# A gated linear attention and a SoLU layer in one kernel: a new order of the work, five states added on VectorE, five squares halved on GpSimd, the last unit in halves

## The chip, the cores and the metric

The kernel runs on one core of a Trainium2 chip. The metric is the time of one execution in microseconds as the device measures it. Runs of one kernel differ by about half a per cent, so the median of several is given. Besides, one execution was profiled: the profile gives the span from the first to the last instruction, and what each engine did in it. The engines are TensorE (in the rows PE, its weight loads PEld), VectorE (DVE), ScalarE (ACT), GpSimd (POOL) and SyncE (SP), which only issues transfers.

## The reference

Two layers. The first goes through 768 steps for each of 4 batches and 8 heads, with a state of 48 x 48 for each head:

```python
for t in range(S):
    kt, vt, rt, wt = (k[:, :, t], v[:, :, t], r[:, :, t], w[:, :, t])
    cur = np.einsum('bhd,bhe->bhde', u[None] * kt, vt)
    y[:, :, t] = np.einsum('bhd,bhde->bhe', rt, state + cur)
    state = wt[:, :, :, None] * state + np.einsum('bhd,bhe->bhde', kt, vt)
```

The second takes the 3072 rows of 384 numbers that come out and computes

```python
h = x @ w_in                       # 384 -> 1024
solu = h * softmax(h)
ln = (solu - mean) / np.sqrt(var + 1e-06) * g_ln
return ln @ w_out                  # 1024 -> 384
```

## The kernel before

The sequence is cut into 6 chunks of 128 steps. One chunk of one batch is a *unit*: there are 24, unit i being chunk i // 4 of batch i % 4. Every unit goes through the same stages, and each stage is a small function with a short name.

The attention of a unit: `LW`, `LK`, `LR`, `LV` load w, k, r and v (192 KB each). `lw` takes the logarithm of w (ACT), `cum` adds it up over the steps with two matmuls, `ex` takes the exponential in place in PSUM (ACT), and `kp` multiplies k and r by it (DVE). `krk` and `krr` turn the two on TensorE and `kr` copies them to SBUF, or `kt` does both with a transfer that turns (units 12, 13 and 15 to 23). `M` makes the scores of the chunk, `m` masks them (mostly DVE). `p`, `q` (POOL), `dg` (DVE) and `dv` (POOL) make the term with u. `Y` collects the output of the attention in PSUM: the term with u (through a matmul on the identity in units marked `i`; in units marked `n` DVE adds it in `y`), the old state, and the scores times v. `y` copies it to SBUF.

The state: `S` collects in one PSUM bank the sum of the logarithms, the old state (a matmul on the identity with 384 columns) and k times v; `et` takes an exponential of the sums (ACT, 8 columns), `st` multiplies the bank by it (DVE) and writes the new state as bf16. `Y` and `S` of the next chunk of that batch read it.

The second layer: `X` and `xT` turn y (or `xt`, a transfer). `H` makes the hidden product, transposed, with 24 matmuls of 128 columns (for units 17 to 20 by rows, with `ht` turning afterwards). `e` takes the exponential (ACT), `he` multiplies (DVE), `hq` squares (ACT, 1024 columns). `Oa` and `Ob` make the output in one bank: for each of 8 blocks one matmul of he with 386 columns, one of e with 2 columns, one of hq with 1 column, the last two being sums for the normalization. In units with an `ea` word POOL adds the two halves of e first, and 4 of the 8 matmuls of e fall away. `qm` (DVE), `lv`, `rs` (ACT) make the factor of each row, `o` applies it (ACT or DVE), `out` stores 192 KB. Unit 23 goes through the hidden layer in two halves (`HA`, `EA`, `DA`, `QA`, then `HB`, `EB`, `DB`, `QB`). `hot` is a number of matmuls whose result nobody reads.

The order is written out by hand, in one string of some 890 words, `ORDER`. A loop at the end goes through the words and calls the stage. `InOrder` keeps the instructions of each engine in the order of the words, and also the transfers of SP and ACT among themselves. So a word sets the place of its instruction in its engine's queue; an instruction that waits holds up everything behind it on that engine. The part after the dot says the engine (`a` ACT, `d` DVE, `p` POOL; for loads `g` POOL's queue, `a` ACT's, none SP's), or the PSUM bank (0 to 7). Buffers are rings: 7 for the loads, 10 for lw and vb, 6 for kp, kr and dv, 4 for most others, 3 for p and q.

Of the kernel before, what the change touches and what calls it, by code (L numbers as in the profile page):

```python
# [8 lines left out]
F32 = mybir.dt.float32  # L9
# [15 lines left out]
hot10.1 LV1 LR5 LK6.a dv0 LK5.g m2.d LV2.a LO1 M3.0 S0.7 q3 gw2.a gw3.a hot1.4 LI1 q1 lw6 krk1.6 cum4.2 et0 LV4  # L25
m3.d p2 st0 cum6.0 dg3 gw0.a cum5.4 ex4 S3.7 gw1.a p4 kp4 q2 dv3 krr1 ex6 dg1 LV5.g krk4.3 krr4 ex5 vb1.a Y0.i2
kp6 kr4.d y0.a LI2 et3 X0.2 krk6.3 st3 p6 kr1.a vb2.a LW8 xT0.a kp5 krr6 LI0.a dg2 M1.0 krk5.7 krr5 kr6.a m1.d
S1.2 dv1 M4.4 dv2 Y3.i3 S2.6 gw4.a LK7 gw7.a et2 kr5.d LW7.g et1 m4.d hot1.7 y3.a q4 gw6.a Y1.i3 M6.0 gw5.a st2
Y2.i5 y1.a y2.a vb5.a mn0.4 X2.7 wi0.a vb4.a st1 m6.d wi1.p LR7.g M5.2 X1.0 S5.1 xT2.a S4.6 et5 p5 lw7 LR8.g dg4
ce4.d LK8 LV7 et4 ce2.d wi2.a xT1.d st5 LW10.a st4 X3.5 m5.d LR10.a cum7.0 mc0 ex7 xT3.a ce1.d H0.6 dv4 H1.2 kp7  # L30
LK9.g H3.0 e0 lw8 e1 ce0.d LK10.a he0 he1 lw10 H2.6 ce7.d hq0.a ce3.p krk7.5 ce5.p e3 LV9 e2 LK11 hq1.a ce6.d
Oa0.3 q6 he3 vb7.a krr7 Ob0 LW9.g LV6.g Y4.i4 q5 LV8.g LR9.a he2 dg5 LW11 cum10.1 cum8.6 y4.a Oa1.0 qm0 ex10 lv0
rs0 kr7.d ex8 kp10 LW13.g Ob1 krk10.4 o0.a hq3.a p8 kp8 p7 dv5 Y5.n5 qm1 LR11.g y5.d lv1 M7.2 X4.6 LW15.a m7.d
q7 krr10 LW17 dg7 kr10.d xT4.a q8 dg6 rs1 lw11 p10 Oa3.5 o1.a cum11.6 dg8 hq2.a H4.2 LW12 LR12.a ex11 lw9 kp11
out0 S7.0 et7 Ob3 dv7 Y7.n1 vb6.a out1 cum9.6 LR17 LK15.g Oa2.4 qm3 st7 vb8.p e4 Ob2 he4 lv3 dv6 LK14.g krk8.0
S6.2 X5.3 LK12.a LV10 krr8 LV12.g ex9 lw13 y7.d rs3 o3.a hq4.a kp9 lw12 qm2 Y6.i5 lv2 xT5.d X7.7 krk11.6 LV11
# [10 lines left out]
lv8 vb13.p q13 e11 kp18 dv14 rs8 S15.2 o8.a S13.3 st12 e12 Oa9.0 dv15 he11 et15 lw21 LW20 Y15.n6 hq11.a et13
dg13 LV21 he12 Ob9 LV23.g LV19.g p18 st15 M13.4 LW23 y15.d qm9 dv13 kt16 cum21.1 hq12.a ex21 H10.6 lv9 p16 m13.d
st13 lw19 kp21 Y13.i4 Oa11.3 e10 rs9 o9.a out7 he10 q18 cum19.1 Ob11 dg18 qm11 lw20 Oa12.7 Ob12 ex19 LR22 q16
y13.a kp19 hq10.a M16.1 dg16 S14.5 lv11 Y14.n6 rs11 LV20.g X13.4 LV22.g out8 qm12 lv12 p17 m16.d xT13.d y14.d  # L50
o11.a lw22 S16.0 vb17.p et14 q17 dg17 rs12 st14 o12.a LR23 vb18.a cum20.1 p19 et16 ex20 ea10.p H13.3 q19 e13
xt15 dv17 lw23 kt17 dv16 H15.6 st16 kp20 he13 Oa10.5 xt14 M17.0 kt18 dg19 dv18 e15 cum22.2 Ob10 out9 ex22 vb22.p
Y16.i4 ea13.p he15 kp22 y16.a hq13.a p22 qm10 H14.6 vb20.p M18.3 m17.d p20 S18.2 q20 lv10 m18.d ea15.p e14 kt19
et18 rs10 Y17.n1 o10.a Oa13.0 y17.d kt20 p21 X16.4 Ob13 xT16.a st18 out11 q22 M19.3 xt17 he14 H16.1 hq15.a
Y18.n5 vb23.a e16 m19.d hq14.a Oa15.7 vb19.a dg20 kt21 y18.d qm13 out12 Ob15 ea14.p dv19 M20.4 q21 S17.3 lv13
he16 m20.d qm15 dv20 et17 hq16.a lv15 H17.1 rs13 out10 e17 M21.5 st17 xt18 rs15 ea16.p Oa14.4 m21.d Ob14 he17
o15.a o13.a cum23.5 qm14 LK23 Y20.n3 ex23 Y19.n7 lv14 y20.d y19.d H18.0 rs14 o14.a kp23 kt22 M22.3 e18 dg22
X20.2 vb21.p S19.7 m22.d xT20.a Oa16.6 Y21.n5 ht17 et19 p23 sv17 he18 xt19 hq17.a dv22 H20.2 e20 dg21 Ob16 st19
dv21 y21.d he20 hq18.a H19.0 qm16 e19 sv18 Y22.n4 Oa17.7 y22.d he19 kt23 Ob17 X22.5 sq17 M23.3 xT22.d qm17 m23.d
ht18 xt21 ht20 hq19.a lv16 Oa18.2 lv17 rs16 Ob18 ht19 q23 dg23 H21.0 o16.d sv19 Y23.n3 dv23 out15 hq20.a e21  # L60
y23.d H22.4 Oa20.6 out13 e22 Ob20 sq18 ea21.p Oa19.3 Ob19 he21 rs17 he22 hq21.a sq20 Oa21.1 o17.d sv20 out16
# [39 lines left out]
def kernel(  # L101
# [132 lines left out]

    u_bc = consts.tile([C, H, D], BF16)
# [305 lines left out]

    def hidden_half(part):
# [75 lines left out]
    def scaled_out(i, x):  # L618
        o_ps, rs, o = live[i]["o_ps"], rs_t[i % NWK], o_t[i % NWK]
        if x == "d":  # L620
            dve.tensor_scalar(out=o, in0=o_ps[:, :DM], scalar1=rs, scalar2=None, op0=MULT)
        else:
            act.activation(out=o, in_=o_ps[:, :DM], func=COPY, scale=rs)

    def store(i, x):
        c, b = units[i]
        queue[x].dma_start(out=out[b * S + c * C:b * S + (c + 1) * C, :], in_=o_t[i % NWK])
# [8 lines left out]
        H=hidden, e=hidden_exp, he=hidden_mul, ea=hidden_add, hq=hidden_square, Oa=output_a, Ob=output_b,  # L636
# [39 lines left out]
```

## Time and profile before

| | us |
|---|---|
| median of 3 runs | 145.75 |
| lowest and highest of them | 144.95, 146.58 |
| the profiled execution | 145.05 |
| its span | 143.2 |
| busy: PE, DVE, ACT, POOL | 127.6, 124.0, 122.2, 117.2 |

The rows of a timeline give the start, the time, the engine, the line, the operation, what is written and read (buffer numbers left out), the shapes and a count; in brackets stands the idle time of the engine ahead of it and what ended it. Nearly every row has line 86, since all instructions are made in one helper there; go by the names. Groups have a count, the busy time, the mean of one in ns, and the idle time ahead of them with what ended it. A view of waits gives who waited for whom: the sum, how often, the longest.

### The profile page before, as it was taken

To read this page: it belongs to the slowest core of one execution; us is meant where nothing else is said; L and a number is where in the kernel's file an instruction comes from. 1 tells how busy PE (TensorE), PEld (TensorE's weight loads), DVE (VectorE), ACT (ScalarE), POOL (GpSimd) and SP (SyncE) were. 2 spreads that over 40 slices of the span, in tenths; PEclk is the share of its full clock that TensorE was granted. 3 is DMA by queue.
4 is the path that set the end of the run, shared out by engine and by line. 5 is a ranking of instruction groups with operands and counts; after the bars stand their busy time and mean duration, and the time that the engine had idled before them with its cause. 6 is when DMAs were issued, how large, how long until landed. Compare 5 with 4: busy or idle time off the path is not lost.

```text
span 143.2 us, 4784 instructions
## 1 busy us (share of the span) xinstructions
PE 127.6 (89%) x1886; PEld 94.5 (66%) x1886; DVE 124.0 (87%) x206; ACT 122.2 (85%) x254; POOL 117.2 (82%) x150
## 2 busy tenths in 40 slices
PE   0597956988999999999999999996999999999980
PEld 0145445556967878678987797786778566687750
DVE  6048879979999999999999999999699999888480
ACT  3658799979999999999999989995787887887962
POOL 7999999999999999999999999999994753326000
PEclk9999999999999999999999999999999999999998
DMA  4999999999995999999998999996977863985325
GB/s 93 277 297 347 313 287 381 384 267 240 287 299 118 250 273 314 255 263 163 211 268 215 271 201 252 195 256 99 169 165 80 223 128 79 142 213 180 115 80 197
DMA packets 86488, 31.67 MB, mean 221 GB/s; under 512 B 80153, under 2 KB 84258, under 8 KB 86466
## 3 DMA queue, kind: packets, MB, share of 16 engines
q1 hardware_dynamic: 69330, 20.62, 66.6%
q0 software_dynamic: 2432, 7.47, 16.4%
q10 hardware_dynamic: 14704, 3.28, 10.5%
q8 instruction: 14, 0.23, 0.7%
q14 instruction: 8, 0.07, 0.1%
HBM read 22.03 MB, written 4.72 MB: 187 GB/s over the span
## 4 chain that ended last, share of the span: by engine, by line
PE 51%; POOL 21%; ACT 8%; issue 7%; DVE 5%; DMA 4%; ACTq 0%; POOLq 0%; DVEq 0%
PE ps L86 51%; DMA xT<-y 4%; POOL kr_in L86 4%; POOL p L86 4%; POOL q L86 3%; POOL dv L86 2%; POOL v_in L86 2%; ACT hq L86 2%; POOL w_in L86 2%; ACT e L86 2%; DVE he L86 1%; DVE o L86 1%; ACT o L86 1%; ACT ps L86 1%; DVE m L86 1%
## 5 line engine op out<-in xcount | busy, mean ns | idle before, releaser
L86 PE MATMUL ps<-w,he 128*128 128x386 bf16 (+1 forms) x192 | 42.5, 324 | 0.0
L86 PE MATMUL ps<-xT,win_sb 128*128 128x128 bf16 x480 | 29.6, 219 | 1.4 <-DMA xT<-y 1.2
L86 PEld LDWEIGHTS <-win_sb 128*128 128x128 bf16 x480 | 27.4, 98 | 3.0 <-DMA xT<-y 1.3
L86 POOL TENSOR_TENSOR dv<-vb,dg 128x384 bf16<-128x384 bf16 x24 | 19.8, 829 | 11.8 <-DVE dg L86 8.6
L86 DVE TENSOR_TENSOR kp<-ps,kr_in 128x768 bf16<-128x768 f32 x24 | 22.7, 953 | 6.9 <-DMA kr_in<-in_r_dram 3.8
L86 ACT ACTIVATE e<-ps 128x1024 bf16<-128x1024 f32 (+1 forms) x25 | 24.6, 987 | 4.8 <-PE ps L86 3.8
L86 DVE TENSOR_TENSOR m<-ps,keep 128x1024 bf16<-128x1024 f32 x22 | 26.7, 1218 | 0.9 <-PE ps L86 0.9
L86 DVE TENSOR_TENSOR he<-ps,e 128x1024 bf16<-128x1024 f32 (+1 forms) x21 | 24.5, 1170 | 3.0 <-ACT e L86 2.8
L86 PE MATMUL ps<-one_col,hq 128*128 128x1 bf16 x160 | 26.1, 163 | 0.0
L86 POOL TENSOR_TENSOR p<-kr_in 128x384 bf16<-128x384 f32 x24 | 23.9, 1005 | 0.1
L86 POOL TENSOR_TENSOR q<-p,u_bc 128x384 bf16<-128x384 bf16 x24 | 21.8, 916 | 0.3
L86 PEld LDWEIGHTS <-he 128*128 128x128 bf16 x192 | 18.3, 96 | 4.0
L86 ACT ACTIVATE hq<-he 128x1024 bf16<-128x1024 bf16 (+1 forms) x20 | 20.7, 1033 | 0.0
L86 ACT ACTIVATE ps<-ps 128x768 f32<-128x768 f32 x24 | 19.0, 800 | 1.5 <-PE ps L86 1.4
L86 PEld LDWEIGHTS <-hq 128*128 128x128 bf16 x160 | 14.1, 96 | 8.8
L86 PE MATMUL ps<-inv_col,e 128*128 128x2 bf16 x104 | 17.1, 164 | 0.0
L86 ACT ACTIVATE lw<-w_in 128x384 bf16<-128x384 f32 x24 | 12.3, 519 | 4.2 <-DMA w_in<-in_w_dram 4.2
L86 PEld LDWEIGHTS <-kp 128*128 128x128 bf16 x184 | 12.3, 101 | 4.2 <-DVE kp L86 1.9
L86 PEld LDWEIGHTS <-kr 64*128 64x128 bf16 (+1 forms) x272 | 10.2, 95 | 5.3 <-issue 2.1
L86 DVE TENSOR_REDUCE dg<-q 128x8 f32<-128x384 bf16 x24 | 12.9, 543 | 0.0
L86 DVE TENSOR_TENSOR st<-ps,et 128x384 bf16<-128x384 f32 x20 | 10.8, 551 | 1.4 <-ACT et L86 1.4
L86 POOL DMA_DIRECT2D v_in<-in_v_dram x12 | 10.9, 905 | 0.0
(97 smaller groups left out, 284.9 us busy)
## 6 DMA issues: line engine op xcount, KB each, us to landing
out_dram<-o SPq DMA_DIRECT2D x24, 192.0 KB, 2.7
w_in<-in_w_dram SPq DMA_DIRECT2D x12, 192.0 KB, 5.6
kr_in<-in_k_dram SPq DMA_DIRECT2D x12, 192.0 KB, 5.9
v_in<-in_v_dram POOLq DMA_DIRECT2D x12, 192.0 KB, 4.9
kr_in<-in_r_dram POOLq DMA_DIRECT2D x11, 192.0 KB, 4.5
v_in<-in_v_dram SPq DMA_DIRECT2D x11, 192.0 KB, 4.3
kr_in<-in_r_dram SPq DMA_DIRECT2D x9, 192.0 KB, 4.0
wout_f<-in_moe_w_out_dram SPq DMA_DIRECT2D x2, 768.0 KB, 7.1
```

Source lines behind the costliest of these rows:

```text
L86: made = make(*args, **kwargs)
```

## The change

Five things, of which the first is most of the diff.

1. `ORDER` is replaced as a whole. No load, store or turning transfer changes its queue, nor its place among the others of its queue. What changes is how the words of the engines stand among each other and among the transfers, and for some words the engine or the bank. The y of unit 0 stands ahead of the scores of unit 1, with the copy of u and its matmul at the very start. VectorE loses two `o` (six before, four after) and one `xT` to ScalarE; GpSimd gets two more `vb` and gives one cast of w_in to ScalarE; the other copies change places with no change of the counts. The `ea` of unit 14 falls away.
2. In units 10, 13, 15, 16 and 19 (`S` marked `n`) the matmul that adds the old state falls away. `st` has two instructions on VectorE in its place: it adds the bank and the old state into a new f32 tile in SBUF, and multiplies that by et.
3. In units 10, 13, 14, 16 and 22 a new word `qa` lets GpSimd add the second half of hq to the first, in place (512 columns), and 4 of the 8 matmuls of hq fall away.
4. Unit 23's second output goes through its four blocks three times, first he, then e, then hq, where it took the three of a block together.
5. Unit 23's `o` is made in two halves, one on ScalarE and one on VectorE, and stored by two transfers of 96 KB, one on ScalarE's queue and one on SyncE's.

```diff
-LU0 LR3.g LW3.a LW1.a LW2.g lw3 LR0.a cum3.0 LG0 ih0 ex3 LW0 gs0.7 LK3 LR2.g hot1.2 LV0.g ik0 LK0 lw1 lw0 LV3.g
-gc0 cum0.4 LK2.a us0.6 p0 lw2 LW5.g ex0 kp3 LR1 kp0 cum1.0 cum2.2 krk3.7 krr3 uc0 ex2 q0 ex1 kp2 LK1 LR6.g kp1
-krk0.6 LW4 krr0 krk2.5 krr2 kr0.a lw4 LR4.g vb0.a kr2.d vb3.a p1 M0.3 p3 LO0 LW6 dg0 M2.5 kr3.a LK4 m0.d lw5
...
+LR3.g LU0 LW3.a us0.1 LW2.g LW1.a lw3 uc0 ih0 LR0.a LG0 LW0 LK3 LR2.g cum3.3 ex3 lw0 lw1 gs0.0 LK0 LV0.g cum0.6
+LK2.a kp3 ex0 lw2 LR1 cum1.3 gc0 cum2.1 LK1 kp0 krk3.0 ex1 krr3 krk0.6 ex2 hot1.5 krr0 LW4 LO0 kp2 kr3.a kp1
+LV3.g p0 LW5.g q0 ik0 LW6 kr0.a vb0.a M3.1 LR6.g krk2.5 LK4 krr2 LR4.g p1 vb3.a dg0 M0.3 m3.d kr2.a S0.0 krk1.2
+dv0 krr1 S3.7 q1 M2.5 m0.d LK5.g m2.d p2 kr1.a Y0.i1 q2 p3 lw4 q3 LV1 et0 st0 LR5 hot1.3 y0.a M1.5 m1.d gw1.a
...
+kp19 xt14 X13.3 m16.d qm12 xT13.a lv12 qa10.p S14.4 et16 cum20.0 dg17 st16 H13.2 rs12 o12.a ex20 et14 e13 dg18
+H15.6 LV19.g dv17 ea13.p q20 vb21.a kp20 M17.0 Oa10.5 he13 e15 p19 kt18 cum22.2 st14 ex22 q19 Y16.i4 he15 hq13.a
...
+dv20 S19.n2 y19.d LK23 kt22 qm14 hq16.a cum23.5 dg21 vb22.p et19 Y20.n4 ht17 ex23 qa16.p ea16.p xt19 lv14 rs14
...
+rs21 o19.d out18 HB23.7 o21.d EA23 EB23 qa22.p DA23 out19 qm20 QA23.a lv20 out21 Oa22.0 DB23 Ob22 qm22 QB23.d
+lv22 Oa23.4 rs20 rs22 Ob23 o20.d qm23 o22.a lv23 rs23 o23.a out22 out20 out23.h
...
+    sn_t = ring("sn", 2, [C, H, D], F32)
...
-        s_ps = L["s_ps"] = bank([C, DM + H], F32, x, "s_ps")
+        s_ps = L["s_ps"] = bank([C, DM + H], F32, x[-1], "s_ps")
...
-        if c > 0:
+        L["apart"] = x[0] == "n"
+        if c > 0 and not L["apart"]:
             st = st_t[b][(c - 1) % 2]
             pe.matmul(s_ps[:, :DM], lhsT=ident, rhs=st.rearrange("p h e -> p (h e)"), start=False, stop=False,
                       skip_group_check=True)
...
-        dve.tensor_mul(out=st_t[b][c % 2], in0=live[i]["s_ps"][:, :DM].rearrange("p (h e) -> p h e", h=H), in1=et)
+        total = live[i]["s_ps"][:, :DM].rearrange("p (h e) -> p h e", h=H)
+        if live[i]["apart"]:
+            dve.tensor_add(out=sn_t[i % 2], in0=total, in1=st_t[b][(c - 1) % 2])
+            total = sn_t[i % 2]
+        dve.tensor_mul(out=st_t[b][c % 2], in0=total, in1=et)
...
+    paired = {int(word[2:].split(".")[0]) for word in ORDER.split() if word.startswith("qa")}
+
+    def square_add(i, x):
+        hq = hq_t[i % NWK]
+        pool.tensor_add(out=hq[:, :KF // 2, :], in0=hq[:, :KF // 2, :], in1=hq[:, KF // 2:, :])
...
+    split = "out23.h" in ORDER.split()
...
+        if i == NU - 1 and part and split:
+            for f in range(KF // 2, KF):
+                pe.matmul(o_ps[:, :DM + 2], lhsT=he[:, f, :], rhs=w2[:, f, :], start=False, stop=False,
+                          skip_group_check=True)
...
+            return
...
-            pe.matmul(o_ps[:, DM + 2:], lhsT=hq[:, f, :], rhs=one_col[:, :1], start=False, stop=(f == KF - 1),
-                      skip_group_check=True)
+            if i not in paired:
+                pe.matmul(o_ps[:, DM + 2:], lhsT=hq[:, f, :], rhs=one_col[:, :1], start=False, stop=(f == KF - 1),
+                          skip_group_check=True)
+            elif f % 2 == 0:
+                pe.matmul(o_ps[:, DM + 2:], lhsT=hq[:, f // 2, :], rhs=one_col[:, :1], start=False,
+                          stop=(f == KF - 2), skip_group_check=True)
...
+        if i == NU - 1 and split:
+            act.activation(out=o[:, :DM // 2], in_=o_ps[:, :DM // 2], func=COPY, scale=rs)
+            dve.tensor_scalar(out=o[:, DM // 2:], in0=o_ps[:, DM // 2:DM], scalar1=rs, scalar2=None, op0=MULT)
+            return
...
+        if x == "h":
+            act.dma_start(out=rows[:, :DM // 2], in_=o_t[i % NWK][:, :DM // 2])
+            sp.dma_start(out=rows[:, DM // 2:], in_=o_t[i % NWK][:, DM // 2:])
+            return
```

More of the change, by code (lines that the diff above doesn't have):

```diff
@@ L27 @@
[L27 to L36, printed above, removed]
@@ L47 @@
[L47 to L56, printed above, removed]
@@ L57 @@
[L57 to L61, printed above, removed]
@@ new lines @@
+kt19 st18 o10.a X16.3 M19.4 ea15.p dg20 xT16.a kt20 dv18 LV20.g Ob13 p22 m19.d out11 e14 H16.2 Oa15.4 vb19.p
+he14 dg19 e16 qm13 xt17 Ob15 Y18.n5 S17.7 lv13 LV22.g rs13 he16 p21 y18.d kt21 out12 qm15 M20.2 out10 m20.d
+o13.a hq14.a lv15 H17.0 M21.5 et17 q21 st17 vb20.a rs15 dv19 m21.d qa14.p xt18 Y19.n3 Oa14.7 o15.a Ob14 e17 he17
+dv20 S19.n2 y19.d LK23 kt22 qm14 hq16.a cum23.5 dg21 vb22.p et19 Y20.n4 ht17 ex23 qa16.p ea16.p xt19 lv14 rs14
+o14.a H18.0 e18 q22 p23 y20.d dv21 kp23 M22.3 X20.7 m22.d kt23 he18 Oa16.6 Ob16 xT20.a dg22 qm16 sv18 H20.4
@@ new lines @@
+hq18.a ht18 Y21.n7 st19 dv22 y21.d e20 Y22.n0 lv16 rs16 H19.1 o16.a he20 y22.d e19 xt21 hq17.a he19 Oa17.7 ht20
+Ob17 X22.3 xT22.a M23.4 Oa18.6 q23 Ob18 hq20.a H21.1 hq19.a sv17 sv19 dg23 sq17 m23.d vb23.p sq18 qm18 Y23.n3
+ht19 dv23 qm17 H22.4 lv17 y23.d out15 e21 out13 out16 e22 lv18 ea21.p he21 he22 rs18 Oa19.0 ea22.p hq21.a rs17
+Oa20.3 Ob19 Ob20 sq19 o17.a xt23 sq20 qm19 hq22.a Oa21.4 Ob21 out14 out17 o18.d sv20 HA23.5 qm21 lv19 rs19 lv21
+rs21 o19.d out18 HB23.7 o21.d EA23 EB23 qa22.p DA23 out19 qm20 QA23.a lv20 out21 Oa22.0 DB23 Ob22 qm22 QB23.d
@@ L572, in output @@
         e, he, hq, o_ps = e_t[i % NWK], he_t[i % NWK], hq_t[i % NWK], L["o_ps"]
+        if i == NU - 1 and part and split:
+            for f in range(KF // 2, KF):
+                pe.matmul(o_ps[:, :DM + 2], lhsT=he[:, f, :], rhs=w2[:, f, :], start=False, stop=False,
+                          skip_group_check=True)
+            for f in range(KF // 2, KF):
+                pe.matmul(o_ps[:, DM:DM + 2], lhsT=e[:, f, :], rhs=inv_col, start=False, stop=False,
+                          skip_group_check=True)
+            for f in range(KF // 2, KF):
+                pe.matmul(o_ps[:, DM + 2:], lhsT=hq[:, f, :], rhs=one_col[:, :1], start=False, stop=(f == KF - 1),
+                          skip_group_check=True)
+            return
         for f in range(part * KF // 2, (part + 1) * KF // 2):
@@ L584, in output @@
                           skip_group_check=True)
-            pe.matmul(o_ps[:, DM + 2:], lhsT=hq[:, f, :], rhs=one_col[:, :1], start=False, stop=(f == KF - 1),
-                      skip_group_check=True)
+            if i not in paired:
+                pe.matmul(o_ps[:, DM + 2:], lhsT=hq[:, f, :], rhs=one_col[:, :1], start=False, stop=(f == KF - 1),
+                          skip_group_check=True)
+            elif f % 2 == 0:
+                pe.matmul(o_ps[:, DM + 2:], lhsT=hq[:, f // 2, :], rhs=one_col[:, :1], start=False,
+                          stop=(f == KF - 2), skip_group_check=True)
     def output_a(i, x):
@@ L626, in store @@
         c, b = units[i]
-        queue[x].dma_start(out=out[b * S + c * C:b * S + (c + 1) * C, :], in_=o_t[i % NWK])
+        rows = out[b * S + c * C:b * S + (c + 1) * C, :]
+        if x == "h":
+            act.dma_start(out=rows[:, :DM // 2], in_=o_t[i % NWK][:, :DM // 2])
+            sp.dma_start(out=rows[:, DM // 2:], in_=o_t[i % NWK][:, DM // 2:])
+            return
+        queue[x].dma_start(out=rows, in_=o_t[i % NWK])
     stages = dict(
```

43 lines of the change are left out of this document (27 added, 16 removed).

## The prediction

> **What bounds the kernel now.** I read the page first, then a table of the span cut into stages, then the steps of TensorE, then the waits of VectorE and GpSimd. Engines in the rows: PE is TensorE, DVE VectorE, ACT ScalarE, POOL GpSimd. The page:
>
> ```profile
> span 143.2 us, 4784 instructions
> ...
> PE 51%; POOL 21%; ACT 8%; issue 7%; DVE 5%; DMA 4%; ACTq 0%; POOLq 0%; DVEq 0%
> ```
>
> The chain that ended last runs half its way over PE. The table by stage (start:end, length, then busy us of PE, PE's weight loads, DVE, ACT, POOL; cut at the first kp, 6.9, and the first he, 36.2) says something else:
>
> ```profile
> 0.00:6.90 6.90, 1.83 (x6) 0.62 (x6) 2.22 (x23) 3.50 (x6) 5.70 (x21) 1.00 0.83 180
> 6.90:36.20 29.30, 24.28 (x301) 15.89 (x300) 24.80 (x35) 25.03 (x49) 28.78 (x35) 1.00 1.13 314
> 36.20:100.00 63.80, 62.50 (x1049) 50.54 (x1047) 62.62 (x97) 60.63 (x121) 63.24 (x75) 1.00 1.06 233
> 100.00:130.00 30.00, 30.00 (x437) 21.30 (x435) 27.41 (x40) 24.24 (x53) 17.64 (x21) 1.00 0.78 155
> 130.00:143.20 13.20, 8.97 (x106) 6.19 (x103) 6.91 (x15) 8.77 (x26) 1.82 (x2) 0.95 0.37 129
> ```
>
> From 36.2 to 100 all four engines are full: DVE 62.62 of 63.8 us, POOL 63.24. Before it DVE misses 4.5 us of 29.3; after 100 POOL is half empty, DVE misses 2.6 of 30. PE's number has to be checked against its steps, since matmuls overlap:
>
> ```profile
> 71.35 0.32 PE L86 MATMUL ps<-w,he 128*128 128x386 bf16 x1
> 71.51 0.16 PE L86 MATMUL ps<-inv_col,e 128*128 128x2 bf16 x1
> 71.54 0.16 PE L86 MATMUL ps<-one_col,hq 128*128 128x1 bf16 x1
> 71.56 0.32 PE L86 MATMUL ps<-w,he 128*128 128x386 bf16 x1
> ```
>
> A matmul with 386 columns lets the next one start after 0.16 us, one with one or two columns after 0.02 to 0.03, though each is booked with 0.16 or more. So a busy PE in the table may still be waiting between steps; a busy DVE is not. I read the middle as bound by DVE, with POOL as tight and PE a little less, and the end (after about 118) as set by the store of work that PE still holds.
>
> **The change part by part.** *Transfers.* On each of the three queues that issue them (SP, ACT, POOL) the words that load, store and turn are the same in the same order as before, only the last store is cut in two. So no transfer passes another; what moves is when the engines reach their words.
>
> *The start.* DVE's timeline:
>
> ```profile
> 6.95 0.96 DVE L86 TENSOR_TENSOR kp<-ps,kr_in 128x768 bf16<-128x768 f32 x1 [3.80 <-DMA kr_in<-in_r_dram]
> 9.96 0.96 DVE L86 TENSOR_TENSOR kp<-ps,kr_in 128x768 bf16<-128x768 f32 x1 [2.05 <-ACT ps L86]
> 11.24 2.02 DVE L86 TENSOR_TENSOR kp<-ps,kr_in 128x768 bf16<-128x768 f32 x2 [0.32 <-ACT ps L86]
> 13.18 0.68 DVE L86 COPY kr<-ps 128x1024 bf16<-128x1024 bf16 x1
> 13.77 0.54 DVE L86 TENSOR_REDUCE dg<-q 128x8 f32<-128x384 bf16 x1
> 14.23 2.35 DVE L86 TENSOR_TENSOR m<-ps,keep 128x1024 bf16<-128x1024 f32 x2
> 16.95 1.23 DVE L86 TENSOR_TENSOR m<-ps,keep 128x1024 bf16<-128x1024 f32 x1 [0.37 <-PE ps L86]
> ```
>
> The first product (kp3) waits for unit 3's r, whose load stays first on POOL: 6.95 stays. The 2.05 us ahead of kp0 are ACT's doing:
>
> ```profile
> 8.70 0.52 ACT L86 ACTIVATE lw<-w_in 128x384 bf16<-128x384 f32 x1 [2.08 <-DMA w_in<-in_w_dram]
> 9.13 0.79 ACT L86 ACTIVATE ps<-ps 128x768 f32<-128x768 f32 x1
> ```
>
> lw2 waits for its load and ex0 stands behind it. The new order puts ex0 ahead of lw2, so kp0 can start some 1.5 us sooner (about 8.5). But kp2 is the next word on DVE, and needs lw2 (8.70, still its load), ex1 and ex2: two exponentials of 0.79 after 9.2, so 10.7 to 10.8 in place of 11.24. Half a microsecond of the 1.5 survives there. Behind it kr2's copy goes from DVE to ACT, and Y0 moves ahead of M1 on PE. POOL reaches its dv0 without p3 (a p, 1.0) before it:
>
> ```profile
> 15.00 1.00 POOL L86 TENSOR_TENSOR p<-kr_in 128x384 bf16<-128x384 f32 x1
> 15.95 0.82 POOL L86 TENSOR_TENSOR dv<-vb,dg 128x384 bf16<-128x384 bf16 x1
> ```
>
> so dv0 is done near 15.8 in place of 16.8, and Y0 can follow at about 16. PE waits at Y0 for it, and M1, X0 and cum4 queue behind; I put 0.6 us of new wait before m1. Adding up the gaps of DVE up to the first he, I get about 3.5 us in place of the 4.5 of the table: a gain of 1.0. Bounds: 0 (a gap goes, another comes) and 2.4 (the gaps at kp0 and kp2 both go). The copy of u now stands before ex3 on ACT and its matmul before cum3 on PE; if u's load is late, ex3, lw0 and ex0 are late with it, but kp3 has a load to wait for anyway.
>
> *More work on DVE.* The groups that carry the prices (busy us, mean ns of one):
>
> ```profile
> L86 DVE TENSOR_TENSOR st<-ps,et 128x384 bf16<-128x384 f32 x20 | 10.8, 551 | 1.4 <-ACT et L86 1.4
> ...
> L86 DVE TENSOR_SCALAR o<-ps,rs 128x384 f32<-128x384 f32 x6 | 3.6, 608 | 0.0
> ...
> L86 DVE COPY xT<-ps 128x384 bf16<-128x384 bf16 x8 | 2.8, 353 | 0.2 <-PE ps L86 0.2
> ...
> L86 DVE SCALAR_TENSOR_TENSOR hq<-he 128x512 bf16<-128x512 bf16 x1 | 0.7, 691 | 0.0
> ```
>
> Two m in a row took 2.35, the single one 1.23, so the second costs 1.12: an instruction costs about 0.09 less than its row when another follows. For units 10, 13, 15, 16 and 19 the added tensor_add has the shape of st: 5 x 0.46 = +2.3. The product after it reads SBUF where it read PSUM; the one row with two SBUF inputs (691 ns for 512 columns) less 128 columns at about 1.04 ns (1024 columns of m against 384 of st) gives 558 against 551: no difference. Away go two o (2 x 0.52) and one xT (0.26); the half o of unit 23 adds 0.32. Sum +1.3; bounds +0.9 and +1.9. DVE is full for 64 us and all but one of the adds lie there, so it counts in full.
>
> *A wait that no row of before shows.* While POOL is full it reads SBUF nearly all the time between DMA issues (p, q, dv). Before the change nearly every DVE instruction of size has one input in PSUM. The new product of `sn` and `et` has both in SBUF. If the two engines can't do that at the same time, DVE waits up to one POOL instruction (p: some 1.0 us), each of five times. Bounds 0 and +5.0; the only row with two SBUF inputs (691) ran when POOL had stopped, so it says nothing. I take +0.8, 0.15 a time for a mean wait of 0.3 that I believe by half.
>
> The Trainium skill, SBUF — State Buffer, section "Who interferes with whom", says that a DVE instruction with two SBUF inputs contends with a GpSimd instruction that reads SBUF, and that the loser blocks for the whole instruction. By it the term would be about +2.5 here (half a p each time); no run here shows it yet.
>
> *Less work on PE.* Five matmuls on the identity with 384 columns (0.16 each), 20 of one column (0.02), against four of two columns more for e of unit 14: 0.8 + 0.45 - 0.1 = 1.15 us. Where DVE sets the pace this is worth nothing. After about 118, where PE works off its store, S19 and the squares of 16 and 22 count: -0.3 (bounds 0 and -1.15).
>
> *More work on POOL and ACT.*
>
> ```profile
> L86 POOL TENSOR_TENSOR ea<-e 128x512 bf16<-128x512 bf16 x7 | 8.0, 1148 | 1.4 <-ACT e L86 0.9 <-ACT sq L86 0.6
> ...
> L86 POOL CAST vb<-v_in 128x384 bf16<-128x384 f32 x8 | 4.0, 507 | 0.0
> ...
> L86 POOL CAST win_sb<-win_f 128x1024 bf16<-128x1024 f32 x1 | 1.0, 1043 | 0.0
> ```
>
> Five qa have the shape of ea (5 x 1.15), one ea goes, two vb come (1.0), one cast of w_in goes to ACT (-1.04): +4.6 us. All five qa belong to units whose hq comes after some 90 us, where the table shows POOL emptying; its waits:
>
> ```profile
> POOL dv L86 <- DVE dg L86: 8.6, 3, 4.7
> POOL dv L86 <- ACT vb L86: 3.0, 2, 2.9
> ```
>
> 11.6 us of idle take 4.6 of work: priced 0. Before unit 16's hidden product POOL even has some 1.5 us less to do. Each qa waits for hq from ACT; behind qa10 stand LV19's issue and dv17, behind qa13 ea15, dv18 and LV20, behind qa14 dv20. On PE the output of the unit waits for qa; closest is unit 14, with only Y19 between. If the cover is gone this costs what a rival below says. ACT gets about +1.2 (two o and one xT from DVE, a cast, less two vb); it idles 5.8 us between 100 and 130: 0.
>
> *The end.*
>
> ```profile
> 139.81 0.58 ACT L86 ACTIVATE o<-ps,rs 128x384 f32<-128x384 f32 x1
> ...
> out_dram<-o SPq DMA_DIRECT2D x24, 192.0 KB, 2.7
> ```
>
> o23 in halves on two engines saves about 0.2 of 0.58; half the rows' bytes on each of two queues 0.2 of 2.7 (bounds 0 and 1.3, if it went with the size). Unit 23's second output now asks for hq last; QB23 had no one waiting for it. -0.4.
>
> *Sum*: -1.0 + 1.3 + 0.8 - 0.3 - 0.4 = +0.4 us. The profiled execution took 145.05 us (143.2 of span and 1.85 around it), 0.7 below the median of the three runs, 145.75; on its own time 145.45, on the median's footing 146.1.
>
> **The rivals.** *The start carries through (faster).* In the new order GpSimd's q of a unit mostly stands further ahead of DVE's dg, and y's dv too. If the whole start gain (1.5 and more) holds, and DVE's 2.6 us of idle between 100 and 130 shrink by 1.5, then -1.5 + 1.3 - 1.5 - 0.3 - 0.4 = -2.4: 143.4. For it: those gaps have waits as their cause, and waits are what an order can take away. Against it: in the 64 full microseconds there is 1.2 to win at most, and DVE has more to do.
>
> *DVE and POOL block each other (slower).* At the products of units 10, 13, 15 and 16, all in the full stage up to 100, POOL has next to no idle time. With a wait of half to a whole p each, +2.5 to +5 in place of 0.8, and DVE has no gap to take it: 147.8 to 150.3, say 148.2. It decides from a mean wait of 0.4 us on. For it: a DVE that is full beside a POOL that reads SBUF without a pause. Against it: no row shows such a wait. The section of the Trainium skill named above would have it so.
>
> *POOL becomes late (slower).* Up to dv21 and dv23 it has 2 and 3.4 us more to do. If it has no idle left by unit 16's output, PE stands at the outputs of 14 and 16 behind qa, and dv20 to dv23 come late for y: +1.5, 147.3. It decides when the 11.6 us of waits above fall under about 3 us.
>
> *The booked times are what PE's work costs (much faster).* Then 5 x 0.32 + 16 x 0.16 = 4.2 us go: 141.5. The steps above speak against it.
>
> **How the numbers follow.** My forecast of a change within 1%, 146.1, gets 0.40; the start 0.27; the block 0.20; POOL late 0.10; the booked times 0.03. A measurement of this kernel can tell about 1% (1.5 us) from no change. Of the forecast 0.31 lie within 1%, 0.07 above, 0.02 below; of the start 0.24 below; of the two slower ones 0.28 above: faster 0.29, same 0.36, slower 0.35. The range leaves out the booked times and the upper end of the block: 143.2 to 148.4; the forecast's own is 144.8 to 147.4.
>
> **What would show it.** Right: kp0 at about 8.5 and kp2 at 10.7, the first he at 36.2 as before; st's products 10, 13, 15 and 16 preceded by waits of 0.1 to 0.3 that name POOL or nothing; POOL's waits for dg and vb down from 11.6 to about 7; the last store landing about 0.4 sooner after qm23. Wrong: the first he before 35 with that lead kept at 100; a wait of 0.5 or more at each of the five; or outputs 14 and 16 waiting for qa.

## The result, and the profile after

The changed kernel took 156.6 us in the median of 5 runs (152.6 to 161.3), the kernel before 145.75 beside it (144.3 to 146.6). The ratio is 1.057, with a 95% interval of 1.039 to 1.076: slower, and outside the range I gave. A ratio leaves out runs more than 1.5% above a kernel's fastest; since the changed kernel and some experiments spread by more than that, medians and ranges here are of all runs. The profiled execution was the fastest of them, 152.58 us against 145.05 before, so the traces can speak for 7.5 of the 11 us between the medians; the rest I take up at the end.

The page after, its head and its chain by engines (PE was 51% before):

```profile
span 150.8 us, 4756 instructions
...
PE 23%; DVE 18%; ACT 14%; POOL 14%; DMA 14%; issue 11%; SPq 5%; ACTq 0%; DVEq 0%; POOLq 0%
```

The table by stage at the same cuts, except the end (start:end, length, busy us of PE, PE's weight loads, DVE, ACT, POOL, then PE's clock, DMA share, GB/s):

```profile
6.90:36.20 29.30, 21.86 (x240) 14.42 (x239) 18.67 (x25) 20.30 (x41) 24.96 (x31) 0.88 1.12 304
36.20:100.00 63.80, 60.79 (x996) 48.59 (x994) 61.93 (x94) 59.65 (x115) 59.84 (x71) 1.00 0.92 213
100.00:130.00 30.00, 29.08 (x444) 21.01 (x441) 29.93 (x45) 24.54 (x53) 26.59 (x30) 1.00 0.81 160
```

In the first of these rows VectorE did 18.67 us of work where it did 24.80 before, ScalarE 20.30 where it did 25.03: 6.1 and 4.7 us of work are missing from the start. The rows behind it are as full as before. So I followed marks through both traces (start of the first matmul or product, us):

| mark | before | after | later by |
|---|---|---|---|
| kp0 | 9.96 | 9.47 | -0.5 |
| m1 | 24.62 | 19.16 | -5.5 |
| st2 | 27.48 | 28.79 | +1.3 |
| first hidden product, H0 | 33.26 | 40.59 | +7.3 |
| he8 | 73.63 | 80.28 | +6.7 |
| he10 | 90.81 | 99.17 | +8.4 |
| last output, Ob23 | 137.98 | 145.56 | +7.6 |
| span | 143.2 | 150.8 | +7.6 |

All of it is lost between m1, which comes early (by 5.5 us), and H0. From H0 to the last output the kernel takes 105.0 us, 104.7 before, with all the new operations in it.

What happens there stands in ScalarE's timeline (its DMA issues are ACTq, the time in brackets is idle time and what ended it):

```profile
16.79 1.01 ACT L86 COPY kr<-ps 128x1024 bf16<-128x1024 bf16 x1 [1.69 <-PE ps L86]
...
18.26 0.65 ACTq L86 DMA_DIRECT2D v_in<-in_v_dram  x1
...
26.94 0.51 ACT L86 CAST vb<-v_in 128x384 bf16<-128x384 f32 x1 [2.88 <-DMA v_in<-in_v_dram]
26.95 0.40 ACTq L86 DMA_DIRECT2D win_f<-in_moe_w_in_dram  x1
```

SyncE's timeline has the second half of w_out next to it:

```profile
17.44 1.85 SPq L86 DMA_DIRECT2D wout_f<-in_moe_w_out_dram  x1
```

Unit 2's v (LV2) is issued from ScalarE's queue behind kr1's copy, and kr1 now waits 1.69 us for TensorE. So the load leaves at 18.26, after the second half of w_out (17.44). Before, the same two rows were the other way round:

```profile
16.49 0.60 ACTq L86 DMA_DIRECT2D v_in<-in_v_dram  x1
17.87 0.63 SPq L86 DMA_DIRECT2D wout_f<-in_moe_w_out_dram  x1
```

The DMA table has one row for this load (KB, us from issue to landing), first before, then after:

```profile
v_in<-in_v_dram ACTq DMA_DIRECT2D x1, 192.0 KB, 4.4
```

```profile
v_in<-in_v_dram ACTq DMA_DIRECT2D x1, 192.0 KB, 8.7
```

It is 1.8 us late at the issue and 6.0 us late at the landing (26.9). vb2 stands in ScalarE's order and holds everything behind it; it starts at 26.94, 23.57 before. The third part of w_in (LI0) is issued at 26.95, 23.15 before. The waits that follow (total, times, longest):

```profile
DVE st L86 <- ACT et L86: 3.4, 2, 3.1
DVE w L86 <- ACT mean_sb L86: 3.4, 1, 3.4
PE ps L86 <- ACT vb L86: 2.6, 2, 2.5
```

TensorE idles 2.48 us for vb2, and its clock falls: the page's row of 40 slices of 3.77 us has it at 0.6 and 0.5 in the slices 8 and 9 (26.4 to 33.9 us), and by stretches it is 0.50 from 27.36 to 34.19:

```profile
PEclk9999999659999999999999999999999999999999
```

The eight matmuls of the column mean fall into that stretch, and VectorE's longest wait (3.4 us, for mean_sb) hangs on them. First before, then after:

```profile
28.20 1.47 PE L86 MATMUL ps<-w,mean_w 128*128 128x384 bf16 x8
```

```profile
31.73 2.68 PE L86 MATMUL ps<-w,mean_w 128*128 128x384 bf16 x8
```

So the loss grows behind the load: vb2 is 3.4 us late and H0 7.3. How much of the difference is the clock no run here separates.

### The profile page after: what moved, and what is told of

It reads as the page before. It is cut to its first block, busy times and chain, and to the rows that moved or that the text cites. A ratio compares the mean times of both kernels' runs of the same rounds, so it can differ in the third digit from the quotient of the medians.

```text
span 150.8 us, 4756 instructions
## 1 busy us (share of the span) xinstructions
PE 131.0 (87%) x1865; PEld 96.6 (64%) x1865; DVE 126.4 (84%) x209; ACT 124.4 (82%) x256; POOL 122.6 (81%) x155
## 4 chain that ended last, share of the span: by engine, by line
PE 23%; DVE 18%; ACT 14%; POOL 14%; DMA 14%; issue 11%; SPq 5%; ACTq 0%; DVEq 0%; POOLq 0%
PE ps L86 23%; DMA v_in<-in_v_dram 9%; SPq L86 5%; DMA kr_in<-in_k_dram 5%; DVE m L86 5%; ACT hq L86 4%; DVE kp L86 4%; DVE he L86 3%; POOL kr_in L86 3%; POOL p L86 3%; POOL dv L86 2%; DVE dg L86 2%; ACT e L86 2%; POOL q L86 2%; ACT ps L86 2%
## 5 line engine op out<-in xcount | busy, mean ns | idle before, releaser
L86 POOL TENSOR_TENSOR dv<-vb,dg 128x384 bf16<-128x384 bf16 x24 | 19.9, 834 | 10.9 <-DVE dg L86 9.0
L86 PE MATMUL ps<-one_col,hq 128*128 128x1 bf16 x140 | 22.4, 163 | 0.0
L86 ACT ACTIVATE hq<-he 128x1024 bf16<-128x1024 bf16 (+1 forms) x20 | 20.6, 1032 | 0.6 <-DVE he L86 0.4
L86 PEld LDWEIGHTS <-he 128*128 128x128 bf16 x192 | 17.5, 96 | 3.8
L86 PEld LDWEIGHTS <-hq 128*128 128x128 bf16 x140 | 12.8, 96 | 8.6 <-ACT hq L86 0.2
L86 PE MATMUL ps<-inv_col,e 128*128 128x2 bf16 x112 | 18.0, 165 | 0.0
L86 PEld LDWEIGHTS <-kr 64*128 64x128 bf16 (+1 forms) x272 | 11.4, 97 | 8.6 <-issue 5.3
L86 PEld LDWEIGHTS <-kp 128*128 128x128 bf16 x184 | 12.8, 105 | 6.3 <-issue 4.9
L86 PE MATMUL ps<-kr 64*128 64x128 bf16 x192 | 10.0, 225 | 3.6 <-DVE kp L86 1.8
L86 ACT ACTIVATE o<-ps,rs 128x384 f32<-128x384 f32 (+1 forms) x20 | 11.4, 571 | 0.5
```

The lines of the kernel that those rows point to most:

```text
L86: made = make(*args, **kwargs)
```

## The experiments

**Does the start carry the whole loss? Two hybrids.** e2 has the words of before up to the first output and those of the change behind it, e3 the other way round (in both, kr7's copy stands elsewhere so that banks don't clash).

```diff
 e2:  before's ORDER up to Oa0, then the changed ORDER's remaining words
 e3:  the changed ORDER up to Oa0, then before's remaining words
```

> The words of the kernel before up to the first output (unit 0's), then the words of the changed kernel (states added by VectorE, halved squares, last store in halves). Theory A and B alike, as the whole loss stood in the trace ahead of the first hidden product: first hidden product at 33.3, time 144.5 to 147.0, the same as before within 1%. Rival C2 (the loss at the start hides another: the middle got 7 us of slack from loads that had time to run ahead, and alone it costs 1.5 to 4 us for the added VectorE instructions and their waits): 147.5 to 150.

> The other way round: the words of the changed kernel up to the first output, then those of the kernel before (states added on TensorE, no halved squares, one last store). Theory A and B: the first hidden product at 40 to 41 and the time 152 to 155, the whole loss without any of the new operations. Rival C2: the new operations bring part of the loss, so 148 to 150 here.

e3 took 153.5 us (152.8 to 155.9; ratio 1.042, 1.035 to 1.049), as slow as the changed kernel's better runs, without any of the new operations. In its profiled run, the slowest of the four (155.9), LV2 landed 10.6 us after the issue. So the new start alone costs 6 us and more. e2, however, took 152.5 (150.6 to 153.9; 1.032, 1.023 to 1.042) where theories A and B said 144.5 to 147 and the rival 150 at most: a miss. With H0 at 33.28 as before, it lost 3 us up to he8 and 4 more up to he10. From H0 to the last output e2 takes 112.0 us, the changed kernel 105.0 with nearly the same words. So the new middle costs time of its own, and where the start is late this doesn't show; that loads run ahead in the meantime is my explanation and not shown. In medians over before, e2 has +5.7, e3 +6.7, and both together +10.9.

**Is it the one load? (A) or the order of the start (B)?** In e1 the load is issued earlier in the changed kernel; e4 and e16 issue it later in the kernel before.

```diff
 e1 (changed):  - ... gw1.a LK6.a X0.4 p4 dg1 LV2.a ...    + ... p2 LK6.a LV2.a kr1.a ...
 e4 (before):   - m2.d LV2.a LO1 ...                       + ... gw0.a LV2.a ...
 e16 (before):  - m2.d LV2.a LO1 ...                       + ... ex6 LV2.a ...
```

> The changed kernel with one thing moved: unit 2's load of v (and unit 6's load of k ahead of it) is issued from ScalarE's queue ahead of the copy kr1 in place of behind it, so that it leaves near 15.6 us in place of 18.3 and stands ahead of the second half of w_out. Theory A (the loss is this load, landing 8.7 us after its issue behind the weights, and the waits of vb2, st2, S2 that follow): v of unit 2 lands near 20 to 21, the first hidden product falls from 40.6 to 34 to 36.5, time 146 to 149. Theory B (the new order of the start loses by itself: four copies of kr and three waits of TensorE ahead of M1): v lands sooner, but the first hidden product stays at 38.5 or later, time 151 or more. Theory C (TensorE's clock: the kernel falls back to a cold clock between 26 and 34 us whatever lands): the slices of PEclk of 5 and 6 stay, time 150 or more.

> The kernel before with one word moved: unit 2's load of v leaves ScalarE's queue behind gw0 (near 18.5 to 19 us) in place of ahead of gw2 (16.5), so behind the second half of w_out on the other queue. Nothing else moves. Theory A: it lands near 26 to 27 in place of 20.9, vb2 holds ScalarE about 3 us, the third part of w_in is issued late behind it, the first hidden product is 3 to 7 us later, time 148.5 to 152. Theory B: the landing moves by about the 2 us of the issue, other work covers it, time 145 to 147.

> The kernel before with unit 2's load of v behind ex6 on ScalarE's queue, so that it leaves near 20.5 to 21.5 us and every time behind the second half of w_out and the second and third parts of w_in. Theory A: it lands at 27 to 30, vb2 holds ScalarE 3 to 5 us, the first hidden product at 37 to 40, time 150 to 154 in nearly every execution, with TensorE's granted clock falling between 25 and 35 us. Theory B: under 147.5.

e1: 150.5 us (150.4 to 150.7; 1.024, 1.017 to 1.030), H0 at 36.28: H0 as A said, the time 1.5 above A's range. Two loads moved, LV2 and LK6 ahead of it, bring H0 forward by 4.3 us and the median by 6. The step also overshot (LV2 left at 13.7, not at 15.6): unit 1's v on the other queue landed at 21.9 in place of 20.9, and vb1 waited 1.8 us.

e16: 152.2 us (150.0 to 153.8; 1.032, 1.020 to 1.044). Nothing of the change is in this kernel but one late load, and it shows the same picture as the changed kernel: LV2 leaves at 21.14 and lands at 29.15, H0 at 39.58, the clock of the first stage 0.88, VectorE's work there 18.62. Its table and wait:

```profile
6.90:36.20 29.30, 22.97 (x212) 13.27 (x212) 18.62 (x24) 19.43 (x39) 24.92 (x30) 0.88 1.10 303
```

```profile
ACT vb L84 <- DMA v_in<-in_v_dram: 4.2, 1, 4.2
```

e4, with the issue only 1.7 us later (18.20), is in between: 145.3 to 152.7 in ten runs, median 148.5. Its ratio of 0.995 (0.987 to 1.003) rests, by the rule given above, on three of the ten. In the profiled run (149.2) the load took 7.6 us and H0 came at 36.79. What the other runs did I can't see. So this load, late, is enough for the whole picture in the old order: 3.2% by e16's ratio, 5.9 us in the medians. But e16's load leaves 2.9 us later than the changed kernel's, and e4's, which leaves when that one does, costs 1.7 us in the median. What the load is worth in the changed order is read from e1 and from e10 below.

**With the loads in place, what is left?** e10 has LV2 and LI0 on SyncE's queue, LV2 ahead of LO1; e12 adds the edit of e11 (below); e14, e15 and e17 go on from e12.

```diff
 e10 (changed): - LR5 ... LV2.a ... LO1 ... LI2 ... LI0.a  + LR5 LV2 ... LO1 ... LI2 LI0
 e14 (e12):     - LK18 ... LK22 e12 kt13                   + kt13 LK18 ... LK22 e12
 e15 (e14):     - wi1.a  vb4.p                             + wi1.p  vb4.a
 e17 (e12):     - X3.5 ... Y4.i4                           + hot5.5 X3.5 ... hot4.4 Y4.i4
```

> The changed kernel with unit 2's load of v on SyncE's queue, ahead of the second half of w_out, and the third part of w_in on the same queue behind the second, so that neither stands behind a wait of ScalarE and unit 1's v keeps its place (in the first experiment it landed 2.6 us later, at 21.9, and vb1 waited 1.8 us for it). Theory A: v of unit 2 lands at 21 to 23, no wait over 1 us at vb1, vb2 and st2, the first hidden product at 34.5 to 36, time 148 to 150, spread under 1%. Theory B (the order on TensorE and ScalarE holds the start back, not the loads): the first hidden product at 36.3 or later again, time 150 to 151.

> The changed kernel with both: the loads as in e10_loads and the sum written back into PSUM. Theory C for this order: its five products took 0.56, 0.56, 0.71, 1.43 and 0.63 us, 1.1 us over 0.55 in all, so 0.5 to 1.1 us less than e10_loads. Rival (in this order the hold-ups fall into gaps): the same as e10_loads within 0.4 us.

> As e12_loads_psum (148.8 us; TensorE waits 1.45 us for the turned k of unit 13 ahead of M13), with that turning transfer ahead of the loads LK18, LV18 and LK22 on SyncE's queue, so that it leaves near 80 us in place of 86. If the queue is the cause: no wait at M13, the tenth product of he 1.5 to 3 us sooner against the ninth, time 146 to 147.5. Rival (the middle is bound by VectorE and GpSimd, the wait is only where it shows): the time stays at 148.5 to 149.

> As e14_kt13, with the second cast of w_in back on GpSimd and unit 4's cast of v back on ScalarE, as the kernel before has them. In e12_loads_psum VectorE waits 1.53 us at ce0 for the mean that ScalarE copies behind this cast and y3. If the cast is the cause: ce0 about half a microsecond to one sooner, the first hidden product near 34.5, time 0.5 to 1 below e14_kt13. Rival (GpSimd has no room there, dv4 and p5 come later by as much; or TensorE's cold clock at the first hidden product stays, 0.107 us a step): the same as e14_kt13 within 0.4 us.

> As e12_loads_psum (148.8 us), with nine warming matmuls of 512 columns in the two gaps of TensorE ahead of the first hidden product: five ahead of X3, four ahead of Y4. In e12_loads_psum TensorE is idle 1.04 us ahead of X3 and 0.92 ahead of cum7, and the granted clock is 0.50 from 35.2 to 37.7. If the clock is the cause of the residue: the clock stays at 0.9 or more there, the first product of he comes 2.9 us after the start of the first hidden product in place of 3.8, time 147 to 148. Rival (the clock falls for other reasons, or another engine holds it): no change within 0.5 us.

e10: LV2 landed at 23.2, LI0 at 30.3, no wait above 1 us is left at vb1, vb2 or st2, and H0 came at 35.23. The time was 151.3 (149.0 to 153.8; 1.029, 1.021 to 1.037): H0 as A said, time and spread not. So of the 7.3 us at H0 the loads' places are worth 5.4, and 2.0 stay. e12: 148.8 (148.5 to 149.9; 1.027, 1.020 to 1.034); by the ratios it is 0.2% faster than e10, within both intervals, so what the sum in PSUM is worth in this order stays open. e14 took the wait of 1.45 us at M13 down to 0.65, and 2.0 us appeared at M16 instead: 151.3 (150.0 to 151.9), slower than either theory said. The wait only moved. e15: 149.5 (148.1 to 154.4). ce0 waits 1.53 us for the mean as before, so the cast is not what holds it; why the median is 1.8 us below e14's I don't know.

The clock takes a microsecond behind H0. H0's stretch in e12, then in e17 (x is the count of matmuls, the figure behind POOL the granted clock):

```profile
35.20:37.70 2.50, 2.50 (x25) 2.47 (x24) 2.50 (x4) 1.32 (x2) 2.04 (x3) 0.50 1.06 238
```

```profile
35.20:37.70 2.50, 2.50 (x50) 2.37 (x47) 2.50 (x4) 1.86 (x4) 2.50 (x4) 1.00 1.12 260
```

With nine warming matmuls the clock stays at 1.00, twice as many matmuls run, and he0 comes 2.8 us after H0 in place of 3.8. H0 itself comes at 35.70 in place of 35.23, so the clock isn't what makes it late. That mechanism is shown in the trace; its worth is not: e17 took 147.5 in the profiled run and 149.9 in the median (147.5 to 151.1).

**What do the new operations cost by themselves?** e5 is before with the five states added by VectorE; e11 is e5 with the sum written back into PSUM; e6 is before with the halved squares; e8 is the changed order with e1's loads, the states added by TensorE and the squares not halved (the last unit stays in halves).

```diff
 e5 (before):   - S10.6 S13.3 S15.2 S16.0 S19.7     + S10.n6 S13.n3 S15.n2 S16.n0 S19.n7
 e11 (e5):      - dve.tensor_add(out=sn_t[i % 2], in0=total, in1=st_t[b][(c - 1) % 2])
                - total = sn_t[i % 2]
                + dve.tensor_add(out=total, in0=total, in1=st_t[b][(c - 1) % 2])
 e6 (before):   + qa10.p behind ea10, qa13.p behind p22, qa14.p qa16.p behind ea16, qa22.p behind ea22
 e8 (e1):       - S10.n4 S13.n3 S15.n3 S16.n6 S19.n2, five qa    + S10.4 S13.3 S15.3 S16.6 S19.2
```

> The kernel before, in its own order, with the old state added by VectorE for units 10, 13, 15, 16 and 19 (five tensor_add, five products from SBUF, five matmuls on the identity less). Theory P (the prediction's sum for this part): +2.3 of VectorE for the adds, less what PE is spared, so 146.5 to 148.5 beside 145 to 147 for before, and no wait over 0.4 us at the five products. Theory C (VectorE's product with two inputs in SBUF is held up by GpSimd): products of 1 to 1.6 us or waits of 0.5 to 1.0 ahead of them, +3 to +5. Theory D (the loss of 5 us that the old start with the new rest showed lies in the order of the words behind the start, not in the added work): +1 to +1.5 at most.

> The kernel before with the five states added by VectorE, as in e5_adds (151.5 us; products of 0.89 to 3.51 us), but the sum is written back into PSUM where it came from, so that the product reads PSUM and SBUF and not SBUF twice. Order, number and size of the instructions are the same. Theory C (the product with two inputs in SBUF is held up while GpSimd reads SBUF): the products fall to 0.55 us, time 146.5 to 148. Rival (the added work and the missing slack cost it, not the place of the operand): 150.5 to 152 again.

> The kernel before, in its own order, with the squares of units 10, 13, 14, 16 and 22 halved by GpSimd ahead of their sums on TensorE (five additions of 1.15 us, 20 matmuls of one column less). Theory P: GpSimd's idle time after 100 us takes it, 0 (-0.4 to +0.5). Rival (outputs 14 and 16 and the values dv19 to dv23 come late behind the additions): +1 to +2.

> The changed kernel's order with unit 2's v early (as in the first experiment), and without the new operations: states added on TensorE, squares not halved. What is left is the order alone. Theory D (order): about as slow as with the operations, 149.5 to 151. Theory of the operations (adds and squares cost the middle of the kernel 2 us and more): 147 to 148.5.

e5: 151.5 us (151.4 to 152.1; 1.042, 1.037 to 1.046), far above the +1.3 of my sum. The reason is in one row by form: the product's mean (busy us, mean ns), and beside it the same product from PSUM:

```profile
L84 DVE TENSOR_TENSOR st<-sn,et 128x384 bf16<-128x384 f32 x5 | 8.8, 1752 | 0.2
L84 DVE TENSOR_TENSOR st<-ps,et 128x384 bf16<-128x384 f32 x15 | 8.1, 546 | 0.1
```

Five products take 8.8 us in place of 2.7. There is no wait ahead of them (0.2); the instruction itself is long. The longest, in VectorE's timeline, and what GpSimd ran under it:

```profile
88.88 3.51 DVE L84 TENSOR_TENSOR st<-sn,et 128x384 bf16<-128x384 f32 x1
```

```profile
88.69 0.99 POOL L84 TENSOR_TENSOR p<-kr_in 128x384 bf16<-128x384 f32 x1
89.65 1.76 POOL L84 TENSOR_TENSOR q<-p,u_bc 128x384 bf16<-128x384 bf16 x2
91.36 1.80 POOL L84 DMA_DIRECT2D v_in<-in_v_dram  x2
```

The product starts under a p, lasts through that p and two q, and ends 1.0 us after GpSimd has gone over to issuing DMAs (at 92.39). In e11, with the same words and one operand in PSUM, all twenty products are alike again:

```profile
L84 DVE TENSOR_TENSOR st<-ps,et 128x384 bf16<-128x384 f32 x20 | 10.9, 552 | 1.4 <-ACT et L84 1.2
L84 DVE TENSOR_TENSOR ps<-ps,st 128x384 f32<-128x384 f32 x5 | 2.8, 555 | 0.0
```

e11 took 145.95 us (145.0 to 147.1; 1.005, 1.001 to 1.009). Against the runs of before beside them, e5 is 5.7 us above and e11 0.8: where one operand lies is worth some 5 us, and the five additions, less the five matmuls on the identity, cost under one.

e6: 149.8 us (147.7 to 150.3; 1.023, 1.014 to 1.031). In its profiled run TensorE waits at output 14 for the halved squares:

```profile
PE ps L84 <- POOL hq L84: 2.9, 1, 2.9
```

That is the rival I had put at 1 to 2 us, at 4.0 in the medians; qa14 stood behind ea16 here, which the changed order avoids. e8: 152.3 (150.5 to 154.1; 1.041, 1.034 to 1.049), slower than e1 with the operations. In its trace H0 comes at 36.56, and from H0 to the last output it takes 108.7 us, 4.0 more than before with none of the adds and halved squares in it: the order of the middle costs that by itself. The order without its operations is no better than the operations without their order.

**Two single steps.** e9 moves ex0 ahead of lw2 in the kernel before, the step on which my start term stood. e13 takes the changed words only from unit 15's hidden product on.

```diff
 e9 (before):   - p0 lw2 LW5.g ex0 kp3    + p0 ex0 lw2 LW5.g kp3
 e13:           before's ORDER up to H15, then the changed ORDER's remaining words
```

> The kernel before with one word moved: unit 0's exponential ahead of unit 2's logarithm on ScalarE, the step on which the prediction's start term rests. Theory P: the first product kp0 at 8.5 in place of 9.96, kp2 at 10.7 in place of 11.24, and half a microsecond to one of gain, 144.5 to 145.5 beside 145 to 147. Rival (the loads that follow set the pace, so nothing is kept): kp0 sooner, the first hidden product at 33.3 as before, time the same within 0.3%.

> The words of the kernel before up to unit 15's hidden product (near 100 us), then those of the changed kernel: of the new operations the squares of units 10, 13, 14, 16 and 22, the state of 19 and the last store in halves are left. Between the tenth product of he and the last output the changed kernel took 46.4 us, the kernel before 47.2. If that gain belongs to the late part: 144.5 to 145.5, 0.8 below before. Rival (it belongs to loads that had run ahead by then, or the squares come late as in e6_squares): the same or up to 2 us slower.

e9: kp0 came at 8.98, kp2 at 11.31 (11.24 before), H0 at 33.87; ratio 1.000 (0.995 to 1.005). The microsecond at kp0 is gone at the next word. e13: 146.1 (145.4 to 146.9; 1.006, 1.003 to 1.010): the late part has no gain of its own. No version of these beats the kernel before.

## Why the prediction was wrong

*The step that failed* is the one on transfers: "no transfer passes another; what moves is when the engines reach their words", priced at nothing, and with it the start's -1.0 (bounds 0 to -2.4). H0 came at +7.3. Each queue does keep its words' order, but three queues share the DMA engines, and a load's place among the others' is set by when its issuing engine gets to it. The section on the kernel is wrong where it says that the transfers of SP and ACT keep their order among themselves. In both kernels the word LV2 stands ahead of LO1, but `InOrder` marks that tie `NoSync`, and in the changed kernel LO1 left at 17.44 and LV2 at 18.26. I had the rows: LV2 was the only v on ScalarE's queue, issued 1.4 us ahead of 768 KB on SyncE's. And the change puts two more copies of kr ahead of it on ScalarE (kr2, kr1), one of which waits for TensorE; I asked only what kr2's copy costs ScalarE. The Trainium skill, DMA: Bandwidth & Descriptors, section "Queues, rings and completion order", says that a DMA engine takes packets by turns from the queues that have work for it. By it a load that is issued behind a long one on another queue shares the engines with it and need not wait for its end. The trace agrees. LK6 and LV2 are 2080 packets on ScalarE's queue (q10), nearly all of 192 bytes; the w_out part goes in packets of 1536 bytes on SyncE's (q1), from 21.8 on. Packets, MB and share of the engines' time in the changed kernel, from 20 to 22 us and then from 22 to 25.2:

```profile
q10 hardware_dynamic: 1803, 0.34, 84.3%
...
q1 hardware_dynamic: 234, 0.06, 13.8%
```

```profile
q1 hardware_dynamic: 658, 1.24, 99.9%
q10 hardware_dynamic: 254, 0.05, 7.3%
```

So 87% of the two loads had moved by 22 us, and the last packets came singly among w_out's, the very last after w_out's landing (25.2). Before, all 2080 had moved by 20.6, ahead of w_out's first (21.1). It is the tail of the load that is late. Sharing is not all, though: in e16, where LV2 left at 21.14 behind one part of w_out and two of w_in, no packet of it moved until 24.7.

*The start's small steps.* kp0 at 8.5 was 9.47, ended by a load (k of unit 0) and no longer by ScalarE; kp2 at 10.7 was 11.66. I had noted for kp3 only that a load sets it. Y0 did move up (m1 5.5 us sooner), and nothing came of it: H0 stands behind Y4 and cum7 on TensorE and needs the casts of w_in.

*More work on VectorE*, +1.3, held. VectorE's busy time up to Ob23 rose from 122.65 to 124.98, 2.3 us, of which 1.1 are the next term. In the rows by form of the changed kernel:

```profile
L86 DVE TENSOR_TENSOR st<-sn,et 128x384 bf16<-128x384 f32 x5 | 3.9, 776 | 0.2
```

*The port wait*, +0.8, was about right in size for this order (five products at 776 ns less 549: 1.1), by luck, and wrong in form: I looked for idle time ahead of the product, and it is the product that gets longer. The order is why it is so little. Here is st10 in the changed kernel, with GpSimd under it:

```profile
87.34 0.56 DVE L86 TENSOR_TENSOR st<-sn,et 128x384 bf16<-128x384 f32 x1
```

```profile
87.33 1.81 POOL L86 DMA_DIRECT2D kr_in<-in_k_dram  x2
```

Two of its five products lie on GpSimd's DMA issues and take 0.56 us; the others took 0.71, 1.43 and 0.63. In before's order the same five pay 6.0 us (five times 1752 less 546 ns), more than the rival's upper end of 5.0: I had bounded the wait by one p, and GpSimd runs several instructions without a gap. The rival was real, but with 1.1 us in the changed kernel it is not the cause of this result. The rule of the Trainium skill that I had cited there (the page SBUF — State Buffer) is borne out by e5 and e11, except that the loser is held over three instructions, not one.

*PE -0.3, POOL and ACT 0.* GpSimd's waits for dg and vb, on the whole span:

```profile
POOL dv L86 <- DVE dg L86: 9.0, 5, 3.4
...
POOL dv L86 <- ACT vb L86: 1.9, 1, 1.9
```

That is 10.9 us where I expected 7 and before had 11.6; but behind 83 us they fell from 11.5 to 4.1, and the rest came with the late start. No output waits for qa in the changed kernel. The price of 0 held for this order; e6 shows what it hangs on. PE's -0.3 is too small for any run here to show.

*The end*, -0.4, was 0: from Ob23 to the end of the span both kernels take 5.2 us. The two halves run one after the other, not side by side:

```profile
147.40 0.42 ACT L86 ACTIVATE o<-ps,rs 128x192 f32<-128x192 f32 x1
...
147.85 0.42 DVE L86 TENSOR_SCALAR o<-ps,rs 128x192 f32<-128x192 f32 x1 [0.96 <-ACT o L86]
```

*The rest of the sum*: +1.3 +0.8 -0.3 for H0 to Ob23 is 1.8; measured +0.3 behind the late start, and +2.5 in e1, +1.6 in e12, 0.1 in e17, with the start partly mended. That looks fair and is partly luck, since the sum had no term for the new order of the middle: e8 loses 4.0 us there without the operations, and e2, with before's start, 7.3.

*Not settled*: why runs of the changed kernel go up to 161.3 us (the mean granted clock falls from 0.975 to 0.933 with it), and why e10, e15 and e17 still spread by 3.6 to 6.3 us with the loads in place. Only one execution of each has a trace. The 2 us by which H0 stays late in e10 and its followers are also not found. And e2's 7 us in the middle I can place but not name: waits for a load of k, for turned k of unit 13, and VectorE's additions, no single one over 2.7 us. Behind one of them, TensorE's wait of 2.28 us for a turned k at 94.6, its clock is at 0.50 from 95.98 to 99.39, where before has 1.00; what that costs no run shows.

## What to carry to other kernels

An unchanged order on each DMA queue is not an unchanged order of transfers: for every load issued from a compute engine's queue, look what the change puts ahead of it on that engine, what it waits for, and which big transfer on another queue it will then meet. Price an operation that moves both inputs of a VectorE product into SBUF by what GpSimd does without a gap at that moment, and put one operand into PSUM where you can. Costs of parts of such a schedule don't add: here the new order without its operations and the operations without their order were each 4.0 to 6.5 us slower than before.

## What the runs showed of the hardware that I had not expected

- The same 192 KB load took 4.4 us from issue to landing when it left 1.4 us ahead of a 768 KB transfer on another queue, and 7.6 to 10.6 us (e4, e16, the changed kernel, e3) when it left behind it. In the changed kernel 87% of the packets of it and the load ahead of it had moved 4.9 us before it landed.
- A VectorE product with both inputs in SBUF took 0.89 to 3.51 us under GpSimd's p, q, dv and casts in e5, 0.56 us while GpSimd issued DMAs, and 0.55 us with one input in PSUM.
- TensorE's granted clock was 0.50 for 3.41 us in e12 (34.29 to 37.70), behind gaps of 1.04 and 0.92 us; nine matmuls of 512 columns in those gaps kept it at 1.00 (e17). In the changed kernel it was 0.50 for 6.83 us, in e4 for 10.24: one, two and three times the same stretch. The Trainium skill, TensorE: Matmul & The Clock Gate, section "Part 1: The HAM clock gate", says that the gate watches a free-running window of about 3.4 us; the stretches of low clock agree with its length; that it runs free no run here shows.
